# RWKV-5 attention and a cosine router on one core: eight PSUM banks as tiles of their own, scores by head parity, small set-up work moved into the first turns

## The chip, the cores and the metric

The kernel runs on 1 core of a Trainium2 chip. The metric is the device time of one execution in microseconds, the median of 3 runs. Engines are called PE or TensorE, DVE or VectorE, ACT or ScalarE, POOL or GpSimd, SP or SyncE.

## The reference

All is float32. Attention: 4 sequences of 768 steps, 8 heads of 48 columns; per head a 48x48 state is carried from step to step.

```python
for t in range(S):
    cur = einsum('bhd,bhe->bhde', u * k[t], v[t])
    y[t] = einsum('bhd,bhde->bhe', r[t], state + cur)
    state = w * state + einsum('bhd,bhe->bhde', k[t], v[t])
```

Then a router: the 3072 rows of y (8 heads x 48 = 384 columns) are compared by cosine with 8 expert embeddings, divided by tau. Each row goes to its best expert, `relu(x @ w1[e]) @ w2[e]` with 1024 hidden columns, and the result is scaled with the softmax weight of that expert.

## The kernel before

**Attention, 12 turns.** A sequence is cut into 6 chunks of 128 steps. A turn t takes one chunk of two sequences (u = 0, 1); two turns make a chunk of all four. Within a chunk the decay is put into powers: K is scaled by `kpow` (`scale_k`, L268, GpSimd), R and K are transposed (`turn_r` L273, `turn_k` L278, TensorE), R is scaled while it leaves PSUM (`take_r`, L282, VectorE), K is copied out (`take_k`, L286, ScalarE) and scaled once more for the step's own term (`own_k`, L290, GpSimd, gives KuT). `scores` (L303) multiplies 64-wide halves of K and R, once with KT (own = 0) and once with KuT (own = 1). `mask` (L315) and `own_terms` (L321) on VectorE take the scores out of PSUM. `outer` (L333) makes the state's increment; `half_state`, `next_state` add it. One turn later `with_v` (L381) and `with_state` (L401) make the output, in two phases with a tiny ScalarE copy `between` (L370) them; `take_y` (L408) copies it, `turn_y` (L416) transposes it back, `take_x` (L421, ScalarE) copies that to X, `keep_x` stores it. After each second turn `logits` (L443) and, a turn on, `choose`, `ranks` (L516, L517), `places` and `put` (L565) choose experts and make lists of rows; the last of the chain that `ranks` waits for is L496.

**Order.** Each engine runs its instructions in the order in which the program issues them. In attention that order comes from due times written out by hand (`attention`, L587): a turn has 8 units, each step has a due time, and steps are issued sorted by it. All loads go through SP's queue, in that order too.

**PSUM.** The 8 banks of 512 float32 per partition are four tiles of two banks each (L985 to 988): A and B (`pairs`) for the transposes and scores of sequence u = 0 and 1, U for increments and transposed outputs, Y for outputs and the router. In the trace they are bankA, bankB, bankU, bankY. Waits between engines are put in by the framework, from the tiles that an instruction reads and writes. In bankA the halves are `bank[0]` and `bank[1]`: R's transposes lie in the first, K's in the second; scores of even and odd heads lie in the first and second half, own = 0 and own = 1 beside each other.

**Set-up.** `build_first` (L69) runs WAKE = 9 matmuls of ones (L90) into the banks, computes decay powers, turns them (L111) into `kpow`. `build_consts` makes masks and number rows on VectorE and GpSimd. `build_embeddings` (L179) loads the embeddings and tau, takes norms (Square L188 on ScalarE, root L189 on GpSimd, L196 on VectorE) and transposes them (L203, L211, TensorE). `decays` (L164) loads w as a row and checks its range on VectorE. All of this is issued ahead of the first turn.

**Experts, 8 in a row.** `turn_x` (L679) transposes the 512 gathered rows of an expert in three groups of four (L685), into `Y[:, m % 2]`, and VectorE copies each out (L686). `layer1` (L689) has 8 groups of six passes (3 matmuls with a contraction of 128 each, recorded twice in float32; L694), into `bank[f % 4]`, each followed by a Relu on ScalarE (L697). `layer2` (L700) has 4 groups of 16 passes (L705), into `U[:, t % 2]`, each followed by a scaling with the gate on VectorE (L710) and an indirect store by GpSimd (L711). The order per expert is `layer1(e)`, `turn_x(e + 1)`, gathers, `layer2(e)`.

Of the kernel before, what the change touches and what calls it, by code (L numbers as in the profile page):

```python
# [35 lines left out]
WAKE = 9  # L36
# [32 lines left out]
def build_first(k):  # L69
# [19 lines left out]
    for i in range(WAKE):  # L89
        nc.tensor.matmul(k.bank[i % 8], k.ones, wide, start=True, stop=True)  # L90
# [29 lines left out]
    nc.vector.tensor_mul(k.uw, uw, wc)  # L120

# [42 lines left out]
def decays(k):  # L164

    nc, pool = k.nc, k.const
    wrow = k.X[2][0:1, 1]
    nc.sync.dma_start(out=wrow, in_=k.w.rearrange("(o h) d -> o (h d)", o=1))
    lohi = pool.tile([1, 2], F32, name="lohi")
    nc.vector.tensor_reduce(out=lohi[:, 0:1], in_=wrow, axis=AX.X, op=ALU.min)  # L170
    nc.vector.tensor_reduce(out=lohi[:, 1:2], in_=wrow, axis=AX.X, op=ALU.max)
    nc.vector.tensor_scalar(lohi[:, 0:1], lohi[:, 0:1], W_MIN, None, ALU.is_ge)
    nc.vector.tensor_scalar(lohi[:, 1:2], lohi[:, 1:2], W_MAX, None, ALU.is_le)
    k.far = pool.tile([1, 1], F32, name="far")
    nc.vector.tensor_mul(k.far, lohi[:, 0:1], lohi[:, 1:2])
    nc.vector.tensor_scalar(k.far, k.far, -1.0, 1.0, ALU.mult, ALU.add)


def build_embeddings(k):  # L179

    nc, pool = k.nc, k.aconst
    emb = k.X[1][0:E, 0]
    nc.sync.dma_start(out=emb, in_=k.emb)
    tau = pool.tile([E, 1], F32, name="tau")
    nc.sync.dma_start(out=tau, in_=bass.AP(tensor=k.tau.tensor, offset=k.tau.offset, ap=[[0, E], [1, 1]]))
# [29 lines left out]
def rings(k):  # L215
# [19 lines left out]
    k.AT = ring("AT", 2, [128, 2, 2, NP, HC])  # L235
# [35 lines left out]
def turn_r(k, t, u):  # L271
    for p in range(NP):
        k.nc.tensor.transpose(k.bank[2 * u][:, p * C : (p + 1) * C], pair(of(k.R, t)[:, u], p), k.ident)  # L273


def turn_k(k, t, u):
    for p in range(NP):
        k.nc.tensor.transpose(k.bank[2 * u + 1][:, p * C : (p + 1) * C], pair(of(k.Kw, t)[:, u], p), k.ident)  # L278


def take_r(k, t, u):
    k.nc.vector.tensor_mul(of(k.RT, t)[:, u], k.bank[2 * u].rearrange("q (p i) -> q p i", p=NP), k.rpow)  # L282


def take_k(k, t, u):
    k.nc.scalar.copy(of(k.KT, t)[:, u], k.bank[2 * u + 1].rearrange("q (p i) -> q p i", p=NP))  # L286
# [22 lines left out]
def both(k, u, own):  # L309
    a = k.pairs[u].rearrange("q r (o p i) -> q r o p i", o=2, p=NP)  # L310
    return a[:, :, own]


def mask(k, t, u):
    k.nc.vector.tensor_mul(  # L315
        of(k.AT, t)[:, u], both(k, u, 0), k.smask[:, None, None, :].to_broadcast([128, 2, NP, HC])
# [3 lines left out]
def own_terms(k, t, u):  # L320
    k.nc.vector.copy_predicated(  # L321
        of(k.AT, t)[:, u], k.dmask[:, None, None, :].to_broadcast([128, 2, NP, HC]), both(k, u, 1)
# [17 lines left out]
def added(k, s):  # L340
    return k.U[:, s, 0 : 2 * NP * D].rearrange("q (u p d) -> q u p d", u=2, p=NP)
# [21 lines left out]
def y_out(k, par, p, u, s):  # L363
    col = ((u * 2 + p % 2) * 2 + s) * HC
    return k.Y[(p // 2) * HC : (p // 2) * HC + DP, par, col : col + HC]


def between(k, t):

    k.nc.scalar.copy(k.peek[:, :, None], k.Y[:, :, 0:1])  # L370


def with_v(k, t, phase):
    AT, V = of(k.AT, t), of(k.V, t)
    first = phase == 0
    for u in range(2):
        for q in range(2):
            for p in (q, q + 2):
                for s in range(2):
# [3 lines left out]
                        V[halves(s), u, 2 * p + par, :], AT[halves(s), u, par, p, :],  # L383
# [29 lines left out]
def turn_y(k, t, u):  # L413
    YT = of(k.YT, t)
    for g in range(4):
        k.nc.tensor.transpose(k.U[:, u, g * C : (g + 1) * C], YT[:, u, g % 2, g // 2, :], k.ident)  # L416


def take_x(k, t, u):
# [3 lines left out]
        k.U[:, u, :].rearrange("q (g c d) -> q g c d", g=4, c=2)[:, :, :, 0:D],  # L423
# [25 lines left out]
def take_logits(k, c):  # L449
    k.lgT = k.rt.tile([128, C], F32, name="lgT", tag="lgT")  # L450
    k.nc.vector.tensor_copy(k.lgT, k.Y[:, 0, 0:C])


def turn_logits(k, c):
    k.nc.tensor.transpose(k.Y[:, 1, 0:C], k.lgT, k.ident)


def keep_logits(k, c):
    k.lg = k.rt.tile([128, B, E], F32, name="lg", tag="lg")
    k.nc.vector.tensor_copy(k.lg, k.Y[:, 1, 0:C].rearrange("q (b x) -> q b x", b=B)[:, :, 0:E])  # L460
# [52 lines left out]
def ranks(k, c):  # L513
    mm = k.nc.tensor.matmul
    out = k.Y[:, 0, 0 : B * E].rearrange("q (b x) -> q b x", b=B)
# [4 lines left out]
def places(k, c):  # L520
# [3 lines left out]
    nc.vector.tensor_mul(rank, k.Y[:, 0, 0 : B * E].rearrange("q (b x) -> q b x", b=B), k.oh)  # L524
# [37 lines left out]
def put(k, c):  # L562
    out = k.Y[:, 1, 0 : 2 * E * TM]
# [23 lines left out]
def attention(k):  # L587
# [4 lines left out]
    for t in range(TURNS):  # L592
# [5 lines left out]
        for u in range(2):  # L598
# [8 lines left out]
            plan.at(at + 1.0 + 1.4 * u, mask, k, t, u)  # L607
            plan.at(at + 1.7 + 1.4 * u, own_terms, k, t, u)
# [17 lines left out]
        if bp == 1:  # L626
# [13 lines left out]
            plan.at(then + P + 6.4, collect, k, c)  # L640
    for e in range(2):
# [37 lines left out]
def turn_x(k, e):  # L679
    xT = k.xT[e % 2]  # L680
    for m in range(NK):
        ps = k.Y[:, m % 2, :]
# [17 lines left out]
def layer2(k, e, w2):  # L700
    hT = k.hT[e % 2]
    for t in range(TM):
        ps = k.U[:, t % 2, 0:DM]
# [256 lines left out]
def kernel(  # L960
# [37 lines left out]
    with tc.manual_schedule():  # L998
        with ExitStack() as attention_ctx:
# [4 lines left out]
            build_embeddings(n)  # L1004
            decays(n)
# [35 lines left out]
```

## Time and profile before

| what | us |
|---|---|
| median of 3 runs | 648.73 (647.52 to 651.34) |
| profiled execution | 650.4 |
| its span, first to last instruction | 648.5 |
| attention and set-up, until the first layer 1 | 226.2 |
| 8 experts | 410 |
| after the last matmul | 12 |

The profiled execution's own time is 1.9 us over its span; the stages of the table are cut from the span. Times in the trace are microseconds from the span's start. A float32 matmul is recorded as two passes, each with its weight load (PEld); the ends of matmuls are modelled. The chain of work that ended last is followed back from the last instruction, at each step to what released it. "issue" is time in which an engine waited for nothing that the profile shows. A clock of 1.00 is TensorE's full 2.4 GHz.

### The profile page before, as it was taken

To read this page: it belongs to the slowest core of one execution; us is meant where nothing else is said; L and a number is where in the kernel's file an instruction comes from. 1 tells how busy PE (TensorE), PEld (TensorE's weight loads), DVE (VectorE), ACT (ScalarE), POOL (GpSimd) and SP (SyncE) were. 2 spreads that over 40 slices of the span, in tenths; PEclk is the share of its full clock that TensorE was granted. 3 is DMA by queue.
4 is the path that set the end of the run, shared out by engine and by line. 5 is a ranking of instruction groups with operands and counts; after the bars stand their busy time and mean duration, and the time that the engine had idled before them with its cause. 6 is when DMAs were issued, how large, how long until landed. Compare 5 with 4: busy or idle time off the path is not lost.

```text
span 648.5 us, 12201 instructions
## 1 busy us (share of the span) xinstructions
PE 515.1 (79%) x5357; PEld 311.2 (48%) x5357; DVE 157.9 (24%) x412; ACT 94.8 (15%) x205; POOL 135.3 (21%) x163
## 2 busy tenths in 40 slices
PE   6777787768674488898988898889898899889982
PEld 2766677667663234443443443443443453444441
DVE  4653737383854201101000100100110100110010
ACT  1132232223242011011011001001001101101100
POOL 3543242423212520130130130021012010010010
PEclk9797687878796599999999999999999999999997
DMA  9854575953010212042140240322303202000000
GB/s 175 168 110 95 131 181 147 245 135 101 26 53 26 70 35 98 32 137 79 45 150 9 114 137 7 110 88 72 110 27 135 98 35 97 1 24 12 2 26 15
DMA packets 95520, 54.38 MB, mean 84 GB/s; under 512 B 78781, under 2 KB 90110, under 8 KB 95458
## 3 DMA queue, kind: packets, MB, share of 16 engines
q1 hardware_dynamic: 88658, 43.67, 24.6%
q0 software_dynamic: 4096, 9.45, 4.2%
q8 instruction: 44, 0.72, 0.4%
q10 hardware_dynamic: 2704, 0.40, 0.4%
q14 instruction: 18, 0.15, 0.1%
HBM read 45.63 MB, written 11.01 MB: 87 GB/s over the span
## 4 chain that ended last, share of the span: by engine, by line
PE 75%; DVE 9%; issue 8%; ACT 4%; POOL 1%; DMA 0%; POOLq 0%; ACTq 0%; DVEq 0%
PE bankU L705 27%; PE bankA L694 14%; PE bankB L694 13%; ACT hT L697 3%; DVE y L710 2%; PE bankY L685 2%; PE bankA L303 2%; PE bankB L303 2%; PE bankU L333 2%; PE bankY L381 2%; DVE xTe L686 2%; PE bankY L401 2%; PE bankU L416 2%; PE bankA L273 1%; PE bankA L278 1%
## 5 line engine op out<-in xcount | busy, mean ns | idle before, releaser
L705 PE MATMUL bankU<-w,hT 128*128 128x384 f32 x512 | 172.9, 491 | 17.1 <-DVE y L710 17.1
L705 PEld LDWEIGHTS bankU<-w,hT 128*128 128x128 f32 x512 | 94.8, 190 | 91.7 <-DVE y L710 31.8
L711 POOL DMA_INDIRECT out_dram<-y,take x32 | 31.7, 991 | 348.8 <-DVE y L710 348.8
L694 PE MATMUL bankA<-xTe,w 128*128 128x512 f32 x192 | 90.6, 608 | 11.8 <-ACT hT L697 11.8
L694 PE MATMUL bankB<-xTe,w 128*128 128x512 f32 x192 | 89.3, 601 | 11.6 <-ACT hT L697 11.6
L694 PEld LDWEIGHTS bankA<-xTe,w 128*128 128x128 f32 x192 | 35.6, 193 | 62.2 <-issue 35.3
L694 PEld LDWEIGHTS bankB<-xTe,w 128*128 128x128 f32 x192 | 35.2, 190 | 62.4 <-issue 38.3
L686 DVE COPY xTe<-bankY 128x512 f32<-128x512 f32 x24 | 16.6, 691 | 192.8 <-PE bankY L685 192.8
L710 DVE TENSOR_SCALAR y<-bankU,lists 128x384 f32<-128x384 f32 x32 | 19.8, 618 | 171.3 <-PE bankU L705 171.3
L697 ACT ACTIVATE hT<-bankA 128x512 f32<-128x512 f32 x32 | 19.1, 597 | 289.2 <-PE bankA L694 289.2
L416 PE MATMUL bankU<-ident,YT 128*128 128x128 f32 x96 | 19.1, 330 | 23.3 <-ACT X L421 22.4
L672 POOL DMA_INDIRECT G<-xs,take x32 | 32.5, 1017 | 17.3 <-DVE take L582 7.8
L685 PE MATMUL bankY<-ident,G 128*128 128x128 f32 x96 | 17.4, 302 | 19.2 <-DVE xTe L686 12.6
L290 POOL TENSOR_TENSOR KuT<-KT,uw 128x512 f32<-128x512 f32 x24 | 24.6, 1039 | 33.7 <-ACT KT L286 33.7
L697 ACT ACTIVATE hT<-bankB 128x512 f32<-128x512 f32 x32 | 19.1, 597 | 79.3 <-PE bankB L694 79.3
L416 PEld LDWEIGHTS bankU<-ident,YT 128*128 128x128 f32 x96 | 12.7, 165 | 28.3 <-ACT X L421 25.6
L685 PEld LDWEIGHTS bankY<-ident,G 128*128 128x128 f32 x96 | 11.5, 149 | 27.8 <-DVE xTe L686 16.6
L268 POOL TENSOR_TENSOR Kw<-K,kpow 128x384 f32<-128x384 f32 x24 | 23.7, 1006 | 0.0
L333 PE MATMUL bankU<-V,Kw 64*64 64x48 f32 x768 | 17.4, 234 | 7.7 <-issue 7.7
L381 PE MATMUL bankY<-AT,V 64*64 64x64 f32 x768 | 20.6, 246 | 3.2 <-issue 2.6
L360 POOL TENSOR_TENSOR T<-T,wC 128x384 f32<-128x384 f32 x10 | 8.3, 827 | 60.5 <-DVE T L354 60.5
L333 PEld LDWEIGHTS bankU<-V,Kw 64*64 64x64 f32 x768 | 15.9, 151 | 8.4 <-issue 8.4
(168 smaller groups left out, 454.2 us busy)
## 6 DMA issues: line engine op xcount, KB each, us to landing
w<-in_moe_w_dram SPq DMA_DIRECT2D x24, 512.0 KB, 4.6
w<-in_moe_w_dram SPq DMA_DIRECT2D x32, 384.0 KB, 4.7
K<-in_k_dram SPq DMA_DIRECT2D x24, 192.0 KB, 3.6
V<-in_v_dram SPq DMA_DIRECT2D x24, 192.0 KB, 4.0
xs<-X SPq DMA_DIRECT2D x24, 192.0 KB, 2.0
R<-in_r_dram SPq DMA_DIRECT2D x22, 192.0 KB, 4.2
G<-xs,take POOLq DMA_INDIRECT x32, 3.3
out_dram<-y,take POOLq DMA_INDIRECT x32, 2.6
```

The lines of the kernel that those rows point to most:

```text
L303: k.nc.tensor.matmul(out, K[rows, u, p, halves(s)], RT[rows, u, p, halves(s)], start=True, stop=True, skip_group_check=True,)
L333: k.nc.tensor.matmul(k.U[par * DP : (par + 1) * DP, s, u * NP * D + p * D : u * NP * D + (p + 1) * D], Kw[halves(s), u, h, :], V[halves(s) ...
L381: k.nc.tensor.matmul(y_out(k, par, p, u, s), V[halves(s), u, 2 * p + par, :], AT[halves(s), u, par, p, :], start=first and u == 0 and q == ...
L416: k.nc.tensor.transpose(k.U[:, u, g * C : (g + 1) * C], YT[:, u, g % 2, g // 2, :], k.ident)
L672: k.nc.gpsimd.indirect_dma_start(out=G[:, :], out_offset=None, in_=k.xs[:, :], in_offset=IndirectOffsetOnAxis(ap=k.take[:, e, t : t + 1], ...
L685: k.nc.tensor.transpose(ps[:, t * 128 : (t + 1) * 128], G[:, m * 128 : (m + 1) * 128], k.ident)
L686: k.nc.vector.tensor_copy(xT[:, m, :], ps)
L694: k.nc.tensor.matmul(ps, w1[:, m, f * 128 : (f + 1) * 128], xT[:, m, :], start=(m == 0), stop=(m == NK - 1))
L697: k.nc.scalar.activation(hT[:, f, :], ps, ACT.Relu)
L705: k.nc.tensor.matmul(ps, hT[:, f, t * 128 : (t + 1) * 128], w2[:, f, :], start=(f == 0), stop=(f == NF - 1))
L710: k.nc.vector.tensor_scalar_mul(y, ps, gate)
L711: k.nc.gpsimd.indirect_dma_start(out=k.out[:, :], out_offset=IndirectOffsetOnAxis(ap=k.take[:, e, t : t + 1], axis=0), in_=y[:, :], in_off ...
```

## The change

- The four two-bank PSUM tiles become eight tiles of one bank each: D[0], D[1], O[0], O[1], U[0], U[1], Y[0], Y[1]. `bank` lists them in that order. R's transposes go to D[u], K's to O[u]; what was U[:, i] and Y[:, i] is U[i] and Y[i].
- `scores` is called once per own instead of once per sequence: first all own = 0 of both sequences into D[par], then all own = 1 into O[par] (par is the head's parity). `mask` and `own_terms` go by parity: both masks first, then both predicated copies. AT is laid out to suit.
- `between` reads each half of Y with a copy of its own.
- The loads of embeddings, tau and the row of w become `load_small`, with a due time between the loads of turns 1 and 2. The rest of `build_embeddings` gets a due time of 6.2, within the preparation of turn 1, and `decays` one of 14.2, within that of turn 2.
- WAKE goes from 9 to 6, and these matmuls begin with `bank[6]`.

```diff
-WAKE = 9
+WAKE = 6
...
-        nc.tensor.matmul(k.bank[i % 8], k.ones, wide, start=True, stop=True)
+        nc.tensor.matmul(k.bank[(6 + i) % 8], k.ones, wide, start=True, stop=True)
...
+def load_small(k):
+    nc = k.nc
+    nc.sync.dma_start(out=k.X[1][0:E, 0], in_=k.emb)
+    k.tau_col = k.aconst.tile([E, 1], F32, name="tau")
+    nc.sync.dma_start(out=k.tau_col, in_=bass.AP(tensor=k.tau.tensor, offset=k.tau.offset, ap=[[0, E], [1, 1]]))
+    nc.sync.dma_start(out=k.X[2][0:1, 1], in_=k.w.rearrange("(o h) d -> o (h d)", o=1))
...
-        k.nc.tensor.transpose(k.bank[2 * u][:, p * C : (p + 1) * C], pair(of(k.R, t)[:, u], p), k.ident)
+        k.nc.tensor.transpose(k.D[u][:, p * C : (p + 1) * C], pair(of(k.R, t)[:, u], p), k.ident)
...
-        k.nc.tensor.transpose(k.bank[2 * u + 1][:, p * C : (p + 1) * C], pair(of(k.Kw, t)[:, u], p), k.ident)
+        k.nc.tensor.transpose(k.O[u][:, p * C : (p + 1) * C], pair(of(k.Kw, t)[:, u], p), k.ident)
...
-def scores(k, t, u):
-    RT = of(k.RT, t)
-    for own, K in ((0, of(k.KT, t)), (1, of(k.KuT, t))):
+def scores(k, t, own):
+    RT, K, out = of(k.RT, t), of(k.KuT if own else k.KT, t), k.O if own else k.D
+    for u in range(2):
         for p in range(NP):
             for s in range(2):
                 for par in range(2):
                     rows = slice(par * DP, par * DP + D)
-                    out = k.bank[2 * u + par][s * HC : (s + 1) * HC, (own * NP + p) * HC : (own * NP + p + 1) * HC]
+                    col = (u * NP + p) * HC
                     k.nc.tensor.matmul(
-                        out, K[rows, u, p, halves(s)], RT[rows, u, p, halves(s)],
+                        out[par][s * HC : (s + 1) * HC, col : col + HC], K[rows, u, p, halves(s)], RT[rows, u, p, halves(s)],
...
-    k.nc.scalar.copy(k.peek[:, :, None], k.Y[:, :, 0:1])
+    for par in range(2):
+        k.nc.scalar.copy(k.peek[:, par : par + 1], k.Y[par][:, par * HC : par * HC + 1])
...
-            plan.at(at + 1.0 + 1.4 * u, mask, k, t, u)
-            plan.at(at + 1.7 + 1.4 * u, own_terms, k, t, u)
+            plan.at(at + 1.0 + 0.7 * u, mask, k, t, u)
+            plan.at(at + 2.4 + 0.7 * u, own_terms, k, t, u)
...
+    plan.at(-P + 0.4, load_small, k)
+    plan.at(6.2, build_embeddings, k)
+    plan.at(P + 6.2, decays, k)
...
-        ps = k.Y[:, m % 2, :]
+        ps = k.Y[m % 2]
...
-        ps = k.U[:, t % 2, 0:DM]
+        ps = k.U[t % 2][:, 0:DM]
...
-    n.pairs = [psum.tile([128, 2, 512], F32, name=f"bank{x}") for x in "AB"]
-    n.U = psum.tile([128, 2, 512], F32, name="bankU")
-    n.Y = psum.tile([128, 2, 512], F32, name="bankY")
-    n.bank = [t[:, i, :] for t in (*n.pairs, n.U, n.Y) for i in range(2)]
+    n.D, n.O, n.U, n.Y = ([psum.tile([128, 512], F32, name=f"{x}{i}") for i in range(2)] for x in ("ps", "po", "pu", "py"))
+    n.bank = [*n.D, *n.O, *n.U, *n.Y]
...
-            build_embeddings(n)
-            decays(n)
```

The other places follow from these: the remaining readers and writers of U, Y and AT, and the lines in `build_embeddings` and `decays` that issued the loads, are left out here.

## Rows read from the trace of the kernel before

**Rows 1.** Stretches: length, busy time of each engine (instructions), clock, DMA share, GB/s.
```profile
30.15:226.20 196.05, 135.00 (x4123) 122.14 (x4124) 104.96 (x299) 52.97 (x135) 66.47 (x73) 0.80 0.44 111
104.70:109.30 4.60, 4.60 (x179) 4.60 (x182) 4.14 (x18) 0.99 (x4) 0.00 (x0) 0.52 0.60 138
278.90:330.20 51.30, 44.85 (x126) 21.92 (x125) 4.54 (x7) 4.78 (x8) 8.04 (x8) 1.00 0.25 86
```

**Rows 2.** Waits, 222 to 645: who waited for whom, us in total, times, longest.
```profile
PE bankU L705 <- DVE y L710: 17.1, 24, 0.7
...
PE bankY L685 <- DVE xTe L686: 12.6, 16, 0.8
PE bankA L694 <- ACT hT L697: 11.8, 16, 0.8
PE bankB L694 <- ACT hT L697: 11.6, 16, 0.7
```

**Rows 3.** The chain that ended last, one expert: start, length, what.
```profile
536.45 2.59 PE bankA L694 x6
...
539.12 0.61 ACT hT L697
...
539.77 2.84 PE bankA L694 x6
...
561.10 0.45 PE bankY L685 x4
...
562.33 0.67 PE bankY L685 x4
...
564.43 5.18 PE bankU L705 x16
...
588.01 2.59 PE bankA L694 x6
```

**Rows 4.** The same chain, first turn_x, ahead of the first expert.
```profile
222.46 0.70 DVE xTe L686
...
225.11 1.11 PE bankY L685 x4
```

**Rows 5.** The same chain, the two turn_y ahead of scores 7.
```profile
116.30 0.60 PE bankU L416 x4
...
117.46 0.66 PE bankU L416 x4
```

**Rows 6.** Timeline, 98 to 105: start, length, engine, line, operands, [idle before <-releaser].
```profile
98.77 0.69 DVE L282 TENSOR_TENSOR RT<-bankB,rpow 128x512 f32<-128x512 f32 x1 [1.02 <-PE bankB L278]
...
102.93 1.12 PE L416 MATMUL bankU<-ident,YT 128*128 128x128 f32 x4 [3.62 <-ACT X L421]
...
103.31 0.57 DVE L496 TENSOR_TENSOR pre<-pre,oh 128x8 f32<-128x8 f32 x3
...
104.67 1.13 PE L303 MATMUL bankA<-RT,KT 48*64 48x64 f32 x32
```

**Rows 7.** Timeline, 8 to 31: set-up and the first scores of turns 0 and 1.
```profile
8.45 0.52 ACT L188 ACTIVATE X<-X 8x384 f32<-8x384 f32 x1 [2.88 <-DMA X<-in_moe_expert_emb_dram]
...
11.99 0.60 PE L111 MATMUL bankY<-ident,YT 128*128 128x128 f32 x4
...
14.70 0.58 POOL L189 TENSOR_TENSOR emb_nrm<-emb_nrm,half 8x1 f32<-8x1 f32 x1 [9.28 <-DVE half L147]
...
15.88 2.09 POOL L268 TENSOR_TENSOR Kw<-K,kpow 128x384 f32<-128x384 f32 x2
...
18.49 0.48 PE L211 MATMUL bankU<-ident,X 8*128 8x8 f32 x3 [0.73 <-DVE X L207]
...
22.51 1.13 PE L303 MATMUL bankA<-RT,KT 48*64 48x64 f32 x32
...
30.15 0.69 PE L303 MATMUL bankA<-RT,KT 48*64 48x64 f32 x32 [0.64 <-ACT KT L286]
```

**Rows 8.** Waits, 40 to 185: TensorE, nothing shown as releaser, in outer.
```profile
PE bankU L333 <- issue: 6.0, 4, 2.6
```

More of the change, by code (lines that the diff above doesn't have):

```diff
@@ L181, in build_embeddings @@
     nc, pool = k.nc, k.aconst
[L182 to L185, printed above, removed]
+    emb, tau = k.X[1][0:E, 0], k.tau_col
     sq = k.X[1][0:E, 1]
@@ L301, in scores, with mask, own_terms @@
                     rows = slice(par * DP, par * DP + D)
-                    out = k.bank[2 * u + par][s * HC : (s + 1) * HC, (own * NP + p) * HC : (own * NP + p + 1) * HC]
+                    col = (u * NP + p) * HC
                     k.nc.tensor.matmul(
-                        out, K[rows, u, p, halves(s)], RT[rows, u, p, halves(s)],
+                        out[par][s * HC : (s + 1) * HC, col : col + HC], K[rows, u, p, halves(s)], RT[rows, u, p, halves(s)],
                         start=True, stop=True, skip_group_check=True,
                     )
[L309 to L314, printed above, removed]
+def mask(k, t, par):
     k.nc.vector.tensor_mul(
-        of(k.AT, t)[:, u], both(k, u, 0), k.smask[:, None, None, :].to_broadcast([128, 2, NP, HC])
+        of(k.AT, t)[:, par], k.D[par].rearrange("q (x i) -> q x i", i=HC),
+        k.smask[:, None, :].to_broadcast([128, 2 * NP, HC]),
     )
-def own_terms(k, t, u):
+def own_terms(k, t, par):
     k.nc.vector.copy_predicated(
-        of(k.AT, t)[:, u], k.dmask[:, None, None, :].to_broadcast([128, 2, NP, HC]), both(k, u, 1)
+        of(k.AT, t)[:, par], k.dmask[:, None, :].to_broadcast([128, 2 * NP, HC]),
+        k.O[par].rearrange("q (x i) -> q x i", i=HC),
     )
@@ L382, in with_v @@
                         y_out(k, par, p, u, s),
-                        V[halves(s), u, 2 * p + par, :], AT[halves(s), u, par, p, :],
+                        V[halves(s), u, 2 * p + par, :], AT[halves(s), par, u * NP + p, :],
                         start=first and u == 0 and q == 0, stop=phase == 1, skip_group_check=True,
@@ L415, in turn_y @@
     for g in range(4):
-        k.nc.tensor.transpose(k.U[:, u, g * C : (g + 1) * C], YT[:, u, g % 2, g // 2, :], k.ident)
+        k.nc.tensor.transpose(k.U[u][:, g * C : (g + 1) * C], YT[:, u, g % 2, g // 2, :], k.ident)
 def take_x(k, t, u):
@@ L450, in take_logits @@
     k.lgT = k.rt.tile([128, C], F32, name="lgT", tag="lgT")
-    k.nc.vector.tensor_copy(k.lgT, k.Y[:, 0, 0:C])
+    k.nc.vector.tensor_copy(k.lgT, k.Y[0][:, 0:C])
 def turn_logits(k, c):
-    k.nc.tensor.transpose(k.Y[:, 1, 0:C], k.lgT, k.ident)
+    k.nc.tensor.transpose(k.Y[1][:, 0:C], k.lgT, k.ident)
 def keep_logits(k, c):
     k.lg = k.rt.tile([128, B, E], F32, name="lg", tag="lg")
-    k.nc.vector.tensor_copy(k.lg, k.Y[:, 1, 0:C].rearrange("q (b x) -> q b x", b=B)[:, :, 0:E])
+    k.nc.vector.tensor_copy(k.lg, k.Y[1][:, 0:C].rearrange("q (b x) -> q b x", b=B)[:, :, 0:E])
 FULL = [128, B, E]
@@ L514, in ranks @@
     mm = k.nc.tensor.matmul
-    out = k.Y[:, 0, 0 : B * E].rearrange("q (b x) -> q b x", b=B)
+    out = k.Y[0][:, 0 : B * E].rearrange("q (b x) -> q b x", b=B)
     mm(out, k.umask, k.oh, start=True, stop=False)
@@ L562, in put @@
 def put(k, c):
-    out = k.Y[:, 1, 0 : 2 * E * TM]
+    out = k.Y[1][:, 0 : 2 * E * TM]
     for b in range(B):
```

23 lines of the change are left out of this document (11 added, 12 removed).

## The prediction

> **What bounds the kernel now.** I first cut the span into stages. In the attention stage, 30.15 to 226.20, TensorE is busy 135.00 of 196.05 us at a mean clock of 0.80; in one expert, 278.90 to 330.20, it is busy 44.85 of 51.30 us at 1.00, where the next engine, GpSimd, has 8.04 [rows 1]. So TensorE's order of work sets the end, and the experts, eight times 51.56 us, are the larger part. Next come the waits of the expert stage: TensorE stands still 17.1 us for layer 2's gating on VectorE, 12.6 us for the copies of the turned inputs, and 11.8 and 11.6 us for layer 1's Relu on ScalarE [rows 2]. The chain of one expert shows what these waits are. Six passes of one accumulation take 2.59 us; then comes a Relu of 0.61 us; then the next six begin, and take 2.84 us [rows 3]. Both groups write "bankA", but different halves of it: `f % 4` goes through A0, A1, B0, B1. TensorE waits for a read of the half that it does not write. Between pairs, from A to B, there is no such wait: these are 16 + 16 waits in 64 groups, half of them. U (t % 2) and Y (m % 2) show the same in layer 2 and in `turn_x`. So these are waits on a two-bank tile, not on a bank.
>
> **The change, part by part.** The sum is made against the profiled execution, 650.4 us (span 648.5 and 1.9 around it), which lies 1.7 above the median of 648.73.
>
> **Experts.** Layer 1 takes 561.10 - 536.45 = 24.65 us; eight groups without a wait take 8 x 2.59 = 20.72, so 3.93 go [rows 3]. Layer 2 takes 588.01 - 564.43 = 23.58 us; four groups at the 5.18 of the one that waits for nothing take 20.72, so 2.86 go [rows 3]. `turn_x` takes 564.43 - 561.10 = 3.33 us. With two tiles the second four transposes follow at once; the third four need the bank of the first, so they still start when its copy is done, 562.33, and take 0.67: 0.45 + 0.78 + 0.67 = 1.90, so 1.43 go. Layer 2 runs in all eight experts, a covered `turn_x` in seven: 8 x (3.93 + 2.86) + 7 x 1.43 = **64.3 us**. The idle time alone is 17.1 + 12.6 + 11.8 + 11.6 = 53.1, of which about 8 x 0.33 = 2.6 stay for the third four transposes [rows 2]; the rest of the 64.3 is the slower restart behind each wait (2.84 against 2.59). So 50.5 is the low end; I take 64.3, because the chain counts from start to start. What the waits covered: a Relu of 0.61 us now runs beside 2.59 us of the next group, a gating beside 5.18 us; each bank comes round again four or two groups later. Nothing is late next.
>
> The first `turn_x` also loses its waits: the first copy begins at 222.46, when four transposes are done, and layer 1 at 226.22 [rows 4]; with 1.11 us for each of the two fours behind them it would begin at 224.68: **1.5 us**.
>
> **Turns of attention, outputs.** `turn_y` of the second sequence waits for `take_x` of the first: from 116.90 to 117.46 is 0.56 us of TensorE time [rows 5]. U[0] and U[1] apart, it does not. This stands on the path in the turns before scores 2, 3, 5, 7, 9 and 11 and at the last `turn_y`: 7 x 0.56 = **3.9 us**. Below: nothing, if scores then wait for KuT; above: the full gap with the slower restart, 0.8 each.
>
> **Turns with a choice** (before scores 4, 6, 8, 10). Now `take_r` of the second sequence waits for the last `turn_k` and starts at 98.77, the choice's chain on VectorE ends at 103.31 + 0.57 = 103.88, and TensorE meanwhile waits 3.62 us for `take_x`, which stands behind the choice's Exp; scores start at 104.67 [rows 6]. With D and O apart, `take_r` starts one group of transposes earlier (about 0.85), and both `turn_y` are done long before the choice; the ranks end half a us behind the chain, near 103.5. That is 1.2; if GpSimd's work holds the chain back, 0.3. I take 1.0: 4 x 1.0 = **4.0 us**.
>
> **Scores and masks by parity.** The same count of matmuls, of 512-wide masks and of predicated copies; the first 64 no longer wait for KuT. The first mask starts later and the last predicated copy ends as before, and the transposes that it releases come a whole `outer` later. Zero; the cover is `outer` and both `with_v`, and without it the price in a turn is one mask, about the 0.69 of a `take_r` with as many columns [rows 6]. `between` becomes two tiny copies on ScalarE, ahead of the second `with_v`; `outer` covers them except in the last turn, where one costs less than a Square's 0.52 [rows 7]: inside the rounding. `load_small` puts three small transfers behind the loads of turn 1 in SP's queue instead of ahead: those loads come earlier, the loads of turn 2 where they were.
>
> **The start.** Before, the decay powers are turned at 11.99, after the nine warm-up matmuls; three fewer, six passes of about 0.43 (2.59 / 6), bring that to about 9.4. The four transposes take 0.60 and the copy into kpow no more than a `take_r`, so kpow was there by 13.2 and will be near 10.6. `scale_k` started only at 15.88, because the embeddings' root, behind VectorE's constants, stood ahead of it on GpSimd; scores began at 22.51 [rows 7]. Then it starts at 10.6: 2.09 us for it, a transpose and a `take_k` of about 0.6 each, beside VectorE's constants and two `take_r`, let scores begin near 14.5: **8.0 us** earlier. But the embeddings' chain now stands whole between the transposes of turn 1 and its scores: the Square, 0.52 and its read-out, then from the root to the last transpose 14.70 to 18.97, 4.27 [rows 7]: TensorE, whose seven transposes stand ahead of scores 1 in its order, is held 5.0 us: **-5.0**. That is nearly what the start gains; 3.0 remain. Bounds: TensorE idles 5 us there, and in a stretch behind such an idle the clock was 0.52 (the lower of its two levels, 1.2 GHz), 32 score matmuls taking 1.13 against 0.69 at scores 1 [rows 1, 6, 7]; if the clock falls, turn 1's 288 matmuls (nine times 32) cost 9 x 0.44, 4.0 more, and the start gives -1.0. If it stays and KuT's wait of scores 0 is also saved, +6. The range check, six small VectorE instructions in turn 2's preparation, lies beside transposes and scores: zero; uncovered at most three `take_r`, 2.1.
>
> **Given back.** In the dense part of a turn TensorE stops for up to 2.6 us waiting for nothing that the profile shows [rows 8]; I take it that its instructions are not there yet, so that faster work ahead can meet a longer stop. Bounds: nothing, and all of the 7.9 us of the turns. I take **-2.0**, a quarter: most of these stops lie inside the dense part, the gains before it. The Trainium skill, "Runtime: NRT & Kernel Launch", section Instruction fetch mechanics, says that loading is mostly hidden, because instructions are issued more slowly than they arrive. By that rule nothing is handed back, and the sum would be 76.7 and the time 572; the stops of 2.6 us speak for the other reading.
>
> Sum: 64.3 + 1.5 + 3.9 + 4.0 + 3.0 - 2.0 = 74.7; 650.4 - 74.7 = 575.7, less 1.7 to the median: **574 us**.
>
> **Rivals.** (1) Attention gives nothing: the clock falls in turn 1 and the stops take the turns' gains. 650.4 - 65.8 - 1.7 = **583 us**. For it: a mean clock of 0.80 and stops that nothing releases; against: waits of 3.62 and 0.56 us that are not stops. Chance 0.15. (2) The change does not do what it says: the waits in the experts hang on something other than the two-bank tile, and stay. `turn_y` and `take_r` hang on the same kind of tile, so only the start's 3.0 come: 650.4 - 3.0 - 1.7, about **646 us**. For it: the reads and the writes are already in different banks today, so one may ask why they wait at all. Against: A to B never waits. Chance 0.04. (3) Slower: the clock falls in the experts, where TensorE now goes from bank to bank without a rest. Its place is layers 1 and 2; at half clock, work doubles. The gain of 75 is gone once 75 of the experts' 8 x 43.3 = 346 us of full-clock work run at half; if half of it did, +173: about **747 us**. Against: 1.00 in the expert's row with four banks in rotation, and 0.52 only behind long idles [rows 1]. Chance 0.02. The Trainium skill, "TensorE: Matmul & The Clock Gate", section "A second HAM failure mode: psum-queue depth-cycling", tells of a kernel that rotated through PSUM banks and whose clock swung, because TensorE paused briefly between groups. By that rule today's experts with their pauses should swing too; the trace does not show it.
>
> **The numbers.** The forecast has 0.79. The range, 562 to 587: below, the start's +6, 1.2 a choice, nothing given back, and some of the half-clock stretches of attention gone; above, rival 1 and experts that keep a few us of restarts. Rival 1 lies in it; outside are rivals 2 and 3 and the ends of the unknown terms. A change of 0.5%, 3 us, is about what a measurement tells from none. Faster: the forecast and rival 1, 0.94; same: rival 2 without the chance that the start moves it past the 3 us, 0.03; slower: rival 3 and a start that goes wrong with rival 2, 0.03.
>
> **What would show it.** Right: ScalarE's Relu and VectorE's gating vanish from TensorE's waits; an expert takes about 43.3 us from first group to first group; one wait of about 0.3 us is left in each `turn_x`; scores 0 begin near 14.5, and a gap of 5 us stands before scores 1; no TensorE wait for `take_x`. Wrong: waits for L697 or L710 remain, or the clock in the experts is under 1.00.

## The result, and the profile after

The changed kernel takes **576.08 us** (median of 3 runs, 574.21 to 577.44) against 648.73: a ratio of 0.887, 95% interval 0.881 to 0.893. The forecast was 574, range 562 to 587. The profiled execution took 577.44, its span 575.6, where before had 650.4 and 648.5; the stages below are cut from these spans.

From the profile's page of the changed kernel, the granted clock in 40 slices of the span (a 9 is 90% or more), and the costliest matmuls (busy us, mean ns, then idle time ahead of them):

```profile
PEclk9789788987979659999999999999999999999995
...
L710 PE MATMUL pu<-w,hT 128*128 128x384 f32 x512 | 166.4, 486 | 0.0
...
L699 PE MATMUL ps<-xTe,w 128*128 128x512 f32 x192 | 85.6, 596 | 0.0
L699 PE MATMUL po<-xTe,w 128*128 128x512 f32 x192 | 85.0, 592 | 0.0
```

The 896 records of both layers wait for nothing at all: idle 0.0. From the 16th slice on, which is where the experts begin, the clock stays at 9 up to the last slice but one. A stretch of 322 us of experts in the table of windows (length, busy time of each engine, clock, DMA share, GB/s) is where [rows 1] had 44.85 of 51.30 us:

```profile
218.00:540.00 322.00, 319.56 (x916) 166.68 (x915) 31.36 (x50) 37.61 (x63) 53.09 (x53) 1.00 0.24 84
```

The waits of the changed kernel, 200 to 575, that answer to [rows 2]:

```profile
PE py L690 <- issue: 5.1, 1, 5.1
...
PE py L690 <- DVE xTe L691: 2.4, 7, 0.3
```

The 24 waits for the gating, the 32 for the Relu and nine of the 16 for the copies are gone; what is left of the copies is the 0.3 us a `turn_x` that the prediction kept. (The 5.1 us stand ahead of the first `turn_x`, 5.12 before the change.) The chain of one expert of the changed kernel (start, length, what), beside [rows 3]:

```profile
433.65 5.15 PE ps L699 x12
...
449.10 5.15 PE po L699 x12
454.25 0.45 PE py L690 x4
...
454.72 0.70 DVE xTe L691
...
455.47 0.66 PE py L690 x4
456.13 20.64 PE pu L710 x64
```

Layer 1 takes 454.25 - 433.65 = 20.60, `turn_x` 1.88, layer 2 20.64: 43.12 us an expert in place of 51.56, nothing but matmuls and one copy.

Where the 72.9 us of span went, term by term, measured on the two profiled executions:

| stage | predicted | before | after | gain |
|---|---|---|---|---|
| layer 1, 8 times | 31.4 | 24.65 | 20.60 | 32.4 |
| layer 2, 8 times | 22.9 | 23.58 | 20.64 | 23.5 |
| `turn_x`, 7 times | 10.0 | 3.33 | 1.88 | 10.2 |
| first `turn_x`, first transpose to layer 1 | 1.5 | 7.1 | 5.2 | 1.9 |
| turns, scores 2 to first `turn_x` | 5.4 | 178.3 | 172.5 | 5.8 |
| start, until scores 2 | 3.6 | 40.9 | 39.8 | 1.0 |
| after the last matmul | 0 | 12.2 | 14.5 | -2.2 |

(Predicted: the turns are six `turn_y` and four choices less the 2.0 given back; the start has the seventh `turn_y`.) The lines add up to 72.6, and the experts' to 66.1. Two terms are off in a way that the prediction did not see. The first is the start. Timeline of the changed kernel, 10 to 18 (start, length, engine, line, operands, count):

```profile
10.76 2.32 POOL L272 TENSOR_TENSOR Kw<-K,kpow 128x384 f32<-128x384 f32 x2 [4.36 <-DVE kpow L113]
...
11.19 0.95 DVE L117 TENSOR_TENSOR wC<-YT,wc 128x4 f32<-128x4 f32 x1
...
12.14 0.99 DVE L152 COPY smask<-umask 64x64 f32<-64x64 f32 x1
...
13.53 2.04 POOL L294 TENSOR_TENSOR KuT<-KT,uw 128x512 f32<-128x512 f32 x2 [0.45 <-ACT KT L290]
...
13.66 0.95 DVE L159 TENSOR_SCALAR number<-token 128x24 f32<-128x24 int32 x1
...
14.60 1.01 DVE L135 CAST efirst<-efirst_i 128x8 f32<-128x8 int32 x1
...
15.54 1.95 POOL L272 TENSOR_TENSOR Kw<-K,kpow 128x384 f32<-128x384 f32 x2
15.59 1.02 DVE L135 CAST slot<-slot_i 128x128 f32<-128x128 int32 x1
...
16.62 1.22 DVE L286 TENSOR_TENSOR RT<-ps,rpow 128x512 f32<-128x512 f32 x2
...
17.39 2.37 PE L307 MATMUL ps<-RT,KT 48*64 48x64 f32 x61 [3.60 <-DVE RT L286]
```

Here kpow is ready at 10.68, as predicted (10.6), but scores 0 begin at 17.39 and not near 14.5: `take_r` stands behind five small VectorE instructions of about 1 us each. Each of the five ends less than 0.1 us after an instruction of GpSimd does; GpSimd's three pairs above take 2.32, 2.04 and 1.95 us. The other term is the tail. Timeline of the changed kernel behind its last matmuls:

```profile
560.97 0.28 PE L755 MATMUL ps<-cum,ones 128*128 128x8 f32 x2
...
561.70 0.51 DVE L758 TENSOR_SCALAR need<-ps 1x8 f32<-1x8 f32 x6
562.06 0.98 POOL L716 DMA_INDIRECT out_dram<-y,take  x1 [4.18 <-DVE need L758]
...
562.68 0.14 DVE L931 CAST flag<-some 1x1 int32<-1x1 f32 x1
```

Before the change the same two matmuls, which count what the lists could not hold, ran in a gap of the last expert's layer 1, 27 us ahead of the last matmul. Their place is the framework's choice and not that of the hand-written order. Timeline of the kernel before:

```profile
608.91 0.28 PE L750 MATMUL bankA<-cum,ones 128*128 128x8 f32 x2
```

Now they come last, and the flag that the closing branch reads is written 1.5 us after the last matmul's end (561.14 on the chain).

### The profile page after: what moved, and what is told of

Its sections match the earlier page's. It is cut to its first block, busy times and chain, and to the rows that moved or that the text cites. A ratio compares the mean times of both kernels' runs of the same rounds, so it can differ in the third digit from the quotient of the medians.

```text
span 575.6 us, 12262 instructions
## 1 busy us (share of the span) xinstructions
PE 492.3 (86%) x5351; PEld 313.9 (55%) x5351; DVE 158.3 (27%) x412; ACT 94.5 (16%) x217; POOL 136.7 (24%) x163
## 4 chain that ended last, share of the span: by engine, by line
PE 82%; DVE 8%; issue 6%; POOL 1%; DMA 1%; ACT 0%; POOLq 0%; DVEq 0%
PE pu L710 29%; PE ps L699 14%; PE po L699 14%; PE ps L307 3%; PE po L307 3%; PE py L383 3%; PE pu L334 3%; PE py L403 2%; PE ps L277 2%; PE py L690 2%; PE po L282 2%; PE pu L418 1%; PE py L567 1%; PE py L445 1%; DVE xTe L691 1%
## 5 line engine op out<-in xcount | busy, mean ns | idle before, releaser
L710 PE MATMUL pu<-w,hT 128*128 128x384 f32 x512 | 166.4, 486 | 0.0
L710 PEld LDWEIGHTS pu<-w,hT 128*128 128x128 f32 x512 | 96.7, 190 | 66.2 <-issue 0.5
L699 PE MATMUL ps<-xTe,w 128*128 128x512 f32 x192 | 85.6, 596 | 0.0
L699 PE MATMUL po<-xTe,w 128*128 128x512 f32 x192 | 85.0, 592 | 0.0
L715 DVE TENSOR_SCALAR y<-pu,lists 128x384 f32<-128x384 f32 x32 | 19.8, 618 | 165.5 <-PE pu L710 165.5
L699 PEld LDWEIGHTS po<-xTe,w 128*128 128x128 f32 x192 | 36.5, 190 | 45.9 <-issue 45.9
L699 PEld LDWEIGHTS ps<-xTe,w 128*128 128x128 f32 x192 | 36.8, 192 | 44.3 <-issue 42.4
L702 ACT ACTIVATE hT<-ps 128x512 f32<-128x512 f32 x32 | 19.1, 597 | 239.9 <-PE ps L699 218.9
L677 POOL DMA_INDIRECT G<-xs,take x32 | 32.5, 1017 | 17.3 <-issue 9.2
L702 ACT ACTIVATE hT<-po 128x512 f32<-128x512 f32 x32 | 19.1, 597 | 63.3 <-PE po L699 53.4
L383 PE MATMUL py<-AT,V 64*64 64x64 f32 x768 | 21.2, 251 | 5.8 <-issue 5.1
L334 PE MATMUL pu<-V,Kw 64*64 64x48 f32 x768 | 17.5, 238 | 7.0 <-issue 7.0
L383 PEld LDWEIGHTS py<-AT,V 64*64 64x64 f32 x768 | 18.5, 165 | 6.6 <-issue 5.6
```

The source lines that it names most:

```text
L334: k.nc.tensor.matmul(k.U[s][par * DP : (par + 1) * DP, u * NP * D + p * D : u * NP * D + (p + 1) * D], Kw[halves(s), u, h, :], V[halves(s) ...
L383: k.nc.tensor.matmul(y_out(k, par, p, u, s), V[halves(s), u, 2 * p + par, :], AT[halves(s), par, u * NP + p, :], start=first and u == 0 an ...
L677: k.nc.gpsimd.indirect_dma_start(out=G[:, :], out_offset=None, in_=k.xs[:, :], in_offset=IndirectOffsetOnAxis(ap=k.take[:, e, t : t + 1], ...
L699: k.nc.tensor.matmul(ps, w1[:, m, f * 128 : (f + 1) * 128], xT[:, m, :], start=(m == 0), stop=(m == NK - 1))
L702: k.nc.scalar.activation(hT[:, f, :], ps, ACT.Relu)
L710: k.nc.tensor.matmul(ps, hT[:, f, t * 128 : (t + 1) * 128], w2[:, f, :], start=(f == 0), stop=(f == NF - 1))
```

## The experiments

Three theories stood after the result. **A**: the experts' 66 us are waits on two-bank tiles, taken away by tiles of one bank. **B**: the moved set-up gives nothing, because VectorE's constants meet GpSimd's work. **C**: the tail is the late range check. The rivals are named in the expectations. All ratios are to the kernel before, run on the same chip in the same round: its medians are 649.91 us for e1 to e4, 652.35 for e5 to e8 and 648.78 for e9 to e11. The changed kernel was run against its own 648.73 alone, so the edits to it are compared by their ratios. The diffs show the main lines; "..." marks what is left out.

**e1: the set-up put back.**

```diff
-WAKE = 6
+WAKE = 9
...
-        nc.tensor.matmul(k.bank[(6 + i) % 8], k.ones, wide, start=True, stop=True)
+        nc.tensor.matmul(k.bank[i % 8], k.ones, wide, start=True, stop=True)
...
-    plan.at(-P + 0.4, load_small, k)
-    plan.at(6.2, build_embeddings, k)
-    plan.at(P + 6.2, decays, k)
...
+            load_small(n)
+            build_embeddings(n)
+            decays(n)
```

> Eight tiles and parity order as in the kernel after; warm-up, embeddings, range check and their loads as before. If the moved set-up gave the 3.0 us that the prediction put down for it, this takes 579 (576.1 + 3). If it gave nothing, because scores 1 begin at 30.65 after against 30.15 before, this takes 576 or a little less (575 to 576.5), with scores 1 at about 29.5 to 30.

Measured: 575.48 us, 0.886 [0.878, 0.895]. Scores 0 begin at 21.6 and scores 1 at 28.9, scores 2 at 41.3; the changed kernel has 17.4, 30.7 and 39.8. So the move brings scores 0 forward by 4 us, and the embeddings between turns 0 and 1 take it back; in the time nothing remains that the intervals could tell.

**e2: the kernel before with the moved set-up alone** (`load_small` and its three transfers put into it as well).

```diff
-WAKE = 9
+WAKE = 6
...
-        nc.tensor.matmul(k.bank[i % 8], k.ones, wide, start=True, stop=True)
+        nc.tensor.matmul(k.bank[(6 + i) % 8], k.ones, wide, start=True, stop=True)
...
+    plan.at(-P + 0.4, load_small, k)
+    plan.at(6.2, build_embeddings, k)
+    plan.at(P + 6.2, decays, k)
...
-            build_embeddings(n)
-            decays(n)
```

> The kernel before with the moved set-up alone; the four two-bank tiles stay. If the move gave 3.0 us: 645.7. If it gives nothing: 648.5 to 650, scores 0 near 17.5 to 18.5 instead of 22.5 but scores 1 at 30.5 to 31.5, and all waits of the experts as before.

Measured: 648.74 us, 1.000 [0.996, 1.004]. With four pairs of banks the constants are done at 14.47 and scores 0 begin at 15.77, earlier than with eight tiles and earlier than the 17.5 to 18.5 expected; scores 1 begin at 29.2, where 30.5 to 31.5 was expected. The timeline shows why:

```profile
13.94 0.18 DVE L159 TENSOR_SCALAR number<-token 128x24 f32<-128x24 int32 x1
...
14.25 0.22 DVE L135 CAST slot<-slot_i 128x128 f32<-128x128 int32 x1
...
15.13 0.59 ACT L290 COPY KT<-bankA 128x512 f32<-128x512 f32 x1 [9.27 <-DVE RT L286]
...
15.80 2.04 POOL L294 TENSOR_TENSOR KuT<-KT,uw 128x512 f32<-128x512 f32 x2 [2.44 <-ACT KT L290]
```

`take_k` and so GpSimd's `own_k` wait for `take_r` here, since R and K share a tile; GpSimd rests from 13.36 to 15.80, and the same constants take 0.18 and 0.22 in place of 0.95 and 1.02. Eight tiles let `own_k` start at 13.53, into the constants: the tile split and the moved set-up work against each other.

**e3: U and Y as pairs again, D and O apart.**

```diff
-    n.D, n.O, n.U, n.Y = ([psum.tile([128, 512], F32, name=f"{x}{i}") for i in range(2)] for x in ("ps", "po", "pu", "py"))
+    n.D, n.O = ([psum.tile([128, 512], F32, name=f"{x}{i}") for i in range(2)] for x in ("ps", "po"))
+    two = [psum.tile([128, 2, 512], F32, name=x) for x in ("pu", "py")]
+    n.U, n.Y = ([t[:, i, :] for i in range(2)] for t in two)
```

> The kernel after with U and Y as two-bank tiles again, the same banks read and written in the same order. Waits hang on the tile: 24 waits of layer 2 come back with 0.95 each (22.9), turn_x seven times 1.43 (10.0), turn_y seven times 0.56 (3.9), layer 1 has none: 576.1 + 36.8 = 613. Waits hang on the bank, or the gain comes from elsewhere: 576.

Measured: 613.81 us, 0.943 [0.935, 0.951]. Its waits in the experts are the old ones of layer 2 and `turn_x`, and none for layer 1:

```profile
PE pu L710 <- DVE y L715: 17.0, 24, 0.7
PE py L690 <- DVE xTe L691: 12.6, 16, 0.8
```

**e4: the kernel before, with layer 1 going A0, B0, A1, B1.**

```diff
-        ps = k.bank[f % 4]
+        ps = k.bank[(0, 2, 1, 3)[f % 4]]
```

> The kernel before, layer 1 going through A0, B0, A1, B1 in place of A0, A1, B0, B1. Waits hang on the two-bank tile: a Relu is over before its tile comes round again, all 32 waits of layer 1 go, 8 x 3.93 = 31.4: 648.7 - 31.4 = 617. Waits hang on the bank or on ScalarE's pace: each bank still comes every fourth group, so nothing changes: 648.7.

Measured: 618.25 us, 0.949 [0.941, 0.958]. No tile changes, each bank is used as often as before, and the 32 waits for the Relu are gone; the other two stay. Its waits, and its chain through one layer 1 (first and last two of eight groups):

```profile
PE bankU L705 <- DVE y L710: 16.9, 24, 0.7
PE bankY L685 <- DVE xTe L686: 12.6, 16, 0.8
```

```profile
420.37 2.57 PE bankA L694 x6
422.94 2.58 PE bankB L694 x6
...
435.82 2.58 PE bankA L694 x6
438.39 2.58 PE bankB L694 x6
440.97 0.45 PE bankY L685 x4
```

Eight groups take 440.97 - 420.37 = 20.60, the same as with eight tiles. e3 and e4 settle theory A: the wait goes with two uses in a row of one tile, whichever bank of it they touch, and e4 buys almost half of the whole gain with one line.

**e5: late constants.** The number rows, the four casts and the zeroing of `cum` and of the lists, none of which is read before routing, move into turn 3's preparation.

```diff
-    k.nc.vector.tensor_copy(f, i)
+    k.casts.append((f, i))
...
+    plan.at(2 * P + 6.15, late_consts, k)
```

> The kernel after; the number rows, cum and lists of build_consts are written on VectorE in turn 3's preparation (due 22.15) instead of ahead of the first take_r. If scores 0 start at 17.39 and not at 14.5 because these casts stall one after the other behind GpSimd's work (0.95, 1.01 and 1.02 in place of 0.2), they now start near 14.4: 576.1 - 3.0 = 573. If the start is bound elsewhere, or the embeddings' hold behind it takes the gain, 576.

Measured: 568.85 us, 0.870 [0.862, 0.878]; scores 0, 1 and 2 begin at 13.4, 26.3 and 35.9. VectorE's rows of kpow and `take_r`, and TensorE's of scores 0:

```profile
8.97 0.56 DVE L113 COPY kpow<-py 128x384 f32<-128x384 f32 x1 [2.32 <-PE py L111]
...
12.54 1.29 DVE L293 TENSOR_TENSOR RT<-ps,rpow 128x512 f32<-128x512 f32 x2
```

```profile
13.38 0.30 PE L314 MATMUL ps<-RT,KT 48*64 48x64 f32 x2 [0.73 <-ACT KT L297]
```

Now scores 0 wait for KT. From the end of the copy into kpow to scores 0 it is 13.38 - 9.53 = 3.85 us, 3.85 and 3.84 in e8 and e11, which have the same edit; the prediction's 14.5 - 10.6 is 3.9. In the changed kernel it is 17.39 - 10.68 = 6.71, and 6.7 in e3, e6, e7 and e9. Its kpow:

```profile
10.12 0.56 DVE L113 COPY kpow<-py 128x384 f32<-128x384 f32 x1 [3.47 <-PE py L111]
```

Theory B holds: the 2.9 us that were missing from the start stood behind these constants. More than that is not the edit's: in e5 kpow itself is ready 1.15 us earlier, ahead of anything that was changed, and of the 9.1 us between the two profiled executions (577.44 and 568.31) 5.6 lie behind the start of scores 2 (see the spread below).

**e6: late turns of the embeddings.** VectorE's part of the embeddings stays ahead of turn 1, their seven small transposes and the copies go behind turn 1's scores (bank 7 and a free scratch for them).

```diff
...
-    plan.at(6.2, build_embeddings, k)
+    plan.at(6.95, build_embeddings, k)
+    plan.at(P + 6.45, turn_embeddings, k)
```

> The kernel after; the seven small transposes of the embeddings and their copies come a turn later (due 14.45, in place of 6.2), and the rest of the chain behind the second own_k, so TensorE does not wait for the chain ahead of scores 1. If that hold is what eats the start's gain: scores 1 near 26.5 instead of 30.65, 576.1 - 4 = 572. If stops without a releaser or the clock take it back: 575 to 576.

Measured: 571.25 us, 0.873 [0.866, 0.881]. Scores 1 begin at 25.7, 5.0 us earlier, so the hold of 5 us was real; but scores 2 begin at 39.3 against 39.8. Two stops of 1.1 and 1.9 us without a releaser stand in turn 1, and the transposes behind it follow each other at 0.7 to 0.9 us a group, at a clock of 0.54, where e11 has 0.43 to 0.49 at 1.00. The profiled execution is 3.0 us shorter than the changed kernel's (574.43 and 577.44), and 2.9 of that lie in later turns, which this edit does not touch (see the spread below).

**e7: early range check.** `needs` and the flag of the last expert run ahead of its layer 1, with bank 7 for the sum.

```diff
         w1, w2 = k.weights.pop(0)
+        if e == E - 1:
+            any_left(k)
...
```

> The kernel after; the count that decides whether any expert has rows left over (L755 to L931) is issued ahead of the last expert's layer 1, in an idle bank, instead of where the framework puts it, which in the kernel after is behind the last matmul of layer 2. If the stretch from the last matmul to the end grew from 12.2 to 14.5 us because of this: 576.1 - 2.2 = 574. If not: 576.

Measured: 571.45 us, 0.880 [0.871, 0.888]. From the last matmul to the end, 557.33 to 569.6, is 12.3 us, as before the change (12.2); its last store issues at the same distance from the last matmul as in the changed kernel (558.25 - 557.33 = 0.92, and 562.06 - 561.14 = 0.92), so what the tail waited for was the flag. Theory C holds by the traces: the tail is 12.2 to 12.3 us in all seven where the two matmuls run ahead of the last one (before, e2, e3, e4, e7, e8, e11) and 14.2 to 14.6 in all six where they run behind it. In e3 and e4, where layer 1 has no gaps and layer 2 still has, they stand in a gap of layer 2, at 590.39 and 588.47. The time alone would not show it: the interval of e7 overlaps that of the changed kernel.

**e8: e5, e6 and e7 together**, their three diffs and nothing else.

> The three edits together. If each theory holds and they add: 576.1 - 3.0 - 4.0 - 2.2 = 567. If late constants and late transposes share one gain (the earlier turn 0 only waits longer for loads or stops): 570.

Measured: 568.42 us, 0.871 [0.865, 0.878]. Scores 1 begin at 23.5, scores 2 at 36.0, where e5 alone has 26.3 and 35.9: the late turns add nothing on top of the late constants. What they bring at scores 1 goes again by scores 2; a stop of 2.2 us without a releaser stands between the two in e8, and none in e5.

**e9: the order of the scores by sequence again.**

```diff
-def scores(k, t, own):
-    RT, K, out = of(k.RT, t), of(k.KuT if own else k.KT, t), k.O if own else k.D
-    for u in range(2):
+def scores(k, t, u):
+    RT = of(k.RT, t)
+    for K, out in ((of(k.KT, t), k.D), (of(k.KuT, t), k.O)):
```

> The changed kernel, with the score matmuls again in the order of the sequences (both heads' parities of one sequence, then of the other) in place of parity by parity; everything else as changed. Theory (the prediction's zero): TensorE's order of the scores is worth nothing, because own_k is done ahead of the scores in most turns; 576 to 577 us. Rival: scores by parity let 64 matmuls run before KuT is needed; without it each of the 12 turns waits up to 0.6 us at its scores, and the time is 580 to 583 us, with TensorE waits for KuT in the score rows. Between 577 and 580 the spread of the attention stage (4 us between runs) leaves it open.

Measured: 573.92 us, 0.884 [0.879, 0.889], and no wait of TensorE for KuT: the zero of the prediction stands for TensorE's order, the rival's 580 to 583 is out. The order of the masks, the other half of that zero, was not tested apart.

**e10: sixteen small matmuls more ahead of everything.** They test what the stops without a releaser hang on.

```diff
+    for i in range(16):
+        nc.tensor.matmul(k.bank[4][:, 0:8], k.ones, wide[:, 0:8], start=True, stop=True)
```

> The changed kernel with 16 matmuls of 8 columns, which nothing reads, behind the warm-up: some 128 more records of TensorE (weight loads and passes together), about 2 us beside the set-up. Theory A: the stops of 1 to 3 us that nothing releases in the attention stage come at fixed numbers of TensorE's instructions (every stop of the changed kernel stands at a multiple of 256, plus 193, in the count of records), so each stays at such a number, and is found 128 records earlier in the work: the stop in the outer products of one turn moves to another operation. Theory B: they hang on the work (a certain operation of a turn); then they stay at the operations where they are and their counts are off by 128. Time: 575 to 579 us by both.

Measured: 578.12 us in the one run. The sixteen make 64 records and not 128 (32 passes, each with its weight load). Two rows on either side of one stop, timeline of TensorE in the changed kernel, and then in e10:

```profile
85.60 0.39 PE L334 MATMUL pu<-V,Kw 64*64 64x48 f32 x14
88.38 1.31 PE L334 MATMUL pu<-V,Kw 64*64 64x48 f32 x50 [2.39 <-issue]
```

```profile
87.44 0.40 PE L405 MATMUL py<-RT,Tmid 48*48 48x64 f32 x15
90.32 0.77 PE L405 MATMUL py<-RT,Tmid 48*48 48x64 f32 x17 [2.49 <-issue]
```

With the 32 passes ahead of it, the stop lies 17 + 14 = 31 recorded passes earlier in the work, at the same number of the count: record 3777 of TensorE in both traces, counting weight loads, passes and TensorE's semaphore instructions. The same holds of the stops at 1473, 1729, 2241, 5057, 5313, 6081, 6849 and 8129, and each number is 193 over a multiple of 256. The stops hang on the count of TensorE's instructions, not on the work. The trace also has the transfers of the instruction queue, 16 KB each. Between 40 and 190 us the changed kernel passes 30 such numbers. At 13 of them TensorE stops for 0.6 us or more, and each of these stops ends 1.2 to 1.6 us after the end of such a transfer. At three the stop is shorter; at the 14 without a stop the transfer had ended 1.3 to 7.4 us before.

**e11: e5 and e7 without e6**, the two diffs and nothing else.

> The changed kernel with the late constants (e5) and the early range check of the last expert (e7), without the moved turns of the embeddings (e6). Theory: the two gains lie in different stages and add up: start -4 to -7 us against the changed kernel, tail -2.5; 566 to 567 us, ratio 0.869, no slower than e8 with all three, since e6 added nothing on top of e5. Rival: the moved turns of the embeddings do count, and without them this is 569 to 570 us, slower than e8. Told apart only if the intervals allow; the traces' starts of scores 2 (36 us in e5 and e8) and the tails (12 us in e7 and e8) decide.

Measured: 568.50 us, 0.875 [0.871, 0.880]. The tail is 12.3 us as expected, but scores 2 begin at 38.5, not 36, and 566 to 567 was not reached. e5, e8 and e11 can't be told from one another; e11 is faster than the changed kernel, by 0.012 of the time before, some 7.6 us, since their intervals do not meet.

## Why the prediction was right

**Experts.** Right in mechanism and size, and the larger part of the gain: 64.3 predicted, 66.1 measured. The excess comes from eight groups at 20.60 and 20.64 us where 20.72 stood (the 2.59 of a group that waits for nothing was 0.015 too long). Rival 2 (waits on something other than the tile) is out by e3 and e4. Layer 1 alone brings 0.051 of 649.91 us, 33 us, in e4 (31.4 predicted); U and Y together bring 0.943 - 0.887 = 0.056, some 36 us, in e3 (22.9 + 10.0 + 1.5 predicted for the experts alone; the `turn_y` of the turns are in it). Rival 3 (a falling clock) is out: 1.00 in the row of 218 to 540 above, and 1.00 from 235 to 535 in every trace. What the Trainium skill, "TensorE: Matmul & The Clock Gate", section "A second HAM failure mode: psum-queue depth-cycling", tells of, a clock that swings as a kernel goes round PSUM banks, no run here shows.

**Turns.** TensorE's wait for `take_x` is gone, as forecast; with a choice it now waits for the choice's own chain on VectorE. Waits from scores 2 to the first `turn_x`, before and after:

```profile
PE bankU L416 <- ACT X L421: 21.0, 11, 4.8
...
PE bankY L516 <- DVE oh L492: 4.6, 1, 4.6
```

```profile
PE py L518 <- DVE oh L494: 18.7, 5, 4.8
```

Where [rows 5] had a gap of 0.56, the eight transposes are one piece on the chain of the changed kernel:

```profile
111.32 1.02 PE pu L418 x8
```

From the last transposes of K to the scores, turns 5, 7, 9 and 11 take 3.70 us each before and 2.91 after, 0.79 less, where 0.56 was put down and 0.8 as the upper bound; the four turns with a choice take 25.4 and 21.8 in all, 3.7 less, where 4.0 was put down. From scores 2 to the first transposes of the experts the two profiled executions differ by 5.8 us, close to the predicted 5.4. That agreement is partly luck. The same stretch takes 178.3, 180.1 and 179.1 us in before, e2 and e4, and 172.5, 168.1, 167.9, 165.5 and 172.3 in the changed kernel, e1, e7, e9 and e10, none of which edits it but e9. Means 179.2 and 169.3: the turns give about 10 us, between any two traces 6 to 15.

**Given back.** The 10 us are not all the turns' waits. In these traces TensorE's waits for other engines between scores 2 and the first `turn_x` fall from 32.5 to 25.7 us on average, 6.8 less, where the prediction had 7.4. The stops without a releaser (the 5.1 ahead of `turn_x` left out) rise from 17.9, 20.3 and 19.0 us in before, e2 and e4 to between 21.0 and 23.9, about 3 more: so something was handed back, and 2.0 was a little low. The rest is TensorE's own work: the same 3,800 passes keep it busy 122.4 us on average before and 116.0 after, 6.4 less, at clocks of 0.79 to 0.81 against 0.80 to 0.87 (rows under "Spread without an edit" below). The prediction had the clock only as a reason for the low end of its range; whether the change raised it is not shown. In the two profiled executions the waits give 5.7, the stops take 3.9, and the busy time gives 4.1, about the 5.8 in all. The mechanism, instructions that are not there yet, is borne out by e10, where the stops follow the count and the transfers. The Trainium skill, "Runtime: NRT & Kernel Launch", section Instruction fetch mechanics, says that a sequencer loads its instructions in blocks of 256 and that crossing a block is mostly hidden. The block agrees with the spacing of the stops; the hiding holds at 14 of the 30 boundaries of the changed kernel and fails at the others, with single stops of up to 3.0 us.

**The start.** This step failed: "a transpose and a `take_k` of about 0.6 each, beside VectorE's constants and two `take_r`, let scores begin near 14.5". The constants were costed as lying beside GpSimd's work at no price. Three of them beside `own_k` and the second `scale_k` take 0.95 + 1.01 + 1.02 where e2 has 0.18, 0.17 and 0.22: 2.4 us of the 2.9 by which scores 0 came late. e10 has the same tiles and the same order; there `own_k` begins at 17.23, behind nearly all the constants, they take 0.17 to 0.22, and from kpow to scores 0 it is 4.3 us. The other half of the step, 5.0 us of hold for the embeddings, was right: turn 1's transposes end at 25.5 and its scores begin at 30.65, behind these rows of the changed kernel:

```profile
29.24 0.41 PE L207 MATMUL py<-ident,YT 8*128 8x8 f32 x4 [3.74 <-DVE YT L200]
30.38 0.34 PE L215 MATMUL pu<-ident,X 8*128 8x8 f32 x3 [0.73 <-DVE X L211]
30.65 0.66 PE L307 MATMUL ps<-RT,KT 48*64 48x64 f32 x16
```

So 3.0 expected for scores 1 was -0.5 (30.15 [rows 7] to 30.65), inside the bounds of -1.0 to 6. The clock that the lower bound priced did fall behind this hold, though not for long: it is 0.52 from 30.65 to 34.05 and 0.98 from there to 37.05. The 128 score passes of turn 1 take those 3.4 us, against about 2.4 at 1.00 before, so the fall cost 1 us and not 4. e1 and e2 put a number on the whole step from both sides: with eight tiles or with four pairs the moved set-up is worth nothing that the intervals (some 7 and 2.6 us either way) can tell.

**The tail.** "Nothing is late next" missed one thing: the count of what the lists could not hold, which had stood in a gap of the last layer 1, stood behind the last matmul once TensorE had no gaps left. It cost 2.2 us (the tails under e7).

**Sum.** 74.7 predicted, 73.0 between the two profiled times (650.4 and 577.4). The start, 2.6 too high, and the tail, 2.2, are made good in part by the experts' 1.8 and by 0.4 each of the turns and the first `turn_x`. Rival 1, attention that gives nothing at 583, lies above the interval, whose upper end is 0.893 x 648.73 = 579.

## What to carry to other kernels

When the profile shows a writer waiting for a reader of another bank of the same tile, as here, try whether the wait belongs to the tile: give each bank a tile, or, in one line, go through the banks so that neighbours in time lie in different tiles. Before moving small VectorE work beside GpSimd's, price it at up to one GpSimd instruction each (here 1 us in place of 0.2), not at its own length, and put what nobody reads yet behind the first use of the engine. When a change closes the gaps of the busiest engine, look for what had been running in them, above all what the end waits for.

## What was not expected of the hardware

**VectorE beside GpSimd.** Small VectorE instructions of 0.15 to 0.22 us take 0.95 to 1.02 when an instruction of GpSimd is under way, and end about when it does. The Trainium skill, "SBUF — State Buffer", section SBUF: two separate sides, says that GpSimd and VectorE (in some modes, or with two inputs from SBUF) share a port pair, which one holds for a whole instruction while the other is blocked. The rows agree, with the length of one GpSimd instruction (1.02 us) as the price; not every small instruction pays it, as the next one or two slip in before GpSimd's next. Nor do the two `take_r` of the changed kernel, which read PSUM: they take 0.62 and 0.67 us beside the second `scale_k`.

**Spread without an edit.** The turns took 165.5 to 172.5 us in five traces of kernels that share that stage (but for the order of the scores in e9), while an expert took 43.12 in each of those that was read (the changed kernel, e1, e7, e9). The granted clock goes with it. The stretch from scores 2 to the first `turn_x` in before, the changed kernel, e9 and e10 (length, busy time of each engine, clock, DMA share, GB/s):

```profile
40.85:219.13 178.28, 123.11 (x3799) 112.50 (x3799) 98.21 (x288) 49.60 (x128) 54.50 (x62) 0.80 0.44 112
```

```profile
39.82:212.31 172.49, 119.04 (x3799) 109.98 (x3799) 97.69 (x295) 49.63 (x140) 55.62 (x63) 0.83 0.46 117
```

```profile
43.17:208.71 165.54, 111.45 (x3800) 102.89 (x3799) 97.80 (x295) 49.60 (x140) 55.55 (x63) 0.87 0.48 122
```

```profile
40.41:212.74 172.33, 121.92 (x3800) 112.39 (x3799) 98.23 (x295) 49.66 (x140) 55.69 (x63) 0.80 0.46 117
```

The same number of passes keeps TensorE busy for 111 to 122 us; e1 and e7 lie between, 168.1 us at 0.87 and 167.9 at 0.85. At the same clock of 0.80, before and e10 differ by 6.0 us. Gains of a few us in that stage can't be read from one pair of traces; the clock of the stage has to be read beside them. Why the clock is lower in one execution than in the next stays open, and so does why a transfer of instructions comes late in one and in time in the next.
